# Transformer block on one core: row groups of the VectorE heads, measured matmul prices in the planner, and K/Q copies behind the LN roots

## The chip, the core and the metric

The kernel runs on one core of a Trainium2 chip. TensorE (PE) multiplies, ScalarE (ACT), VectorE (DVE) and GpSimd (POOL) work element by element, SyncE (SP) issues the DMAs. Each engine has its own instruction list, runs it in order and waits on semaphores for the others. The metric is the device time of one execution in microseconds, as a median of several runs.

## The reference

A block with layer norm ahead of attention, then layer norm ahead of a gated MLP, bfloat16 in and out, S = 2048, D = 640, 32 heads of 20, Df = 1728:

```
x  = A_x
h  = x + attention(layernorm(x)) @ wo      # softmax(q k^T / sqrt(20)) v, 32 heads
h2 = h + (gelu(n @ w_gate) * (n @ w_up)) @ w_down      # n = layernorm(h)
```

All 2048 queries see all 2048 keys, so there are 32 x 2048 x 2048 exponentials.

## The kernel before

**Tiles.** Heads go in 8 groups of 4, as a head of 20 (with its row for the bound, 21) fits a row group of 32 partitions. The queries are cut into 7 chunks (SIZES: 512, 512, 256, 256, 256, 128, 128). A chunk of 512 takes one head group per slot, a chunk of 256 two, a chunk of 128 four, so that there are 32 slots. The smallest piece of attention is a tile of 128 keys x 512 columns in one PSUM bank: `(slot, group, key block, j)`, where j is the head in its group and also the row group of PE that its score matmul uses (`qk_mms`, L934-935, `tile_position=(32 * j, 0)`). Tiles of unlike j can go through PE side by side, those of the same j can't.

**Units.** Tiles are laid out in one long list and cut into 703 units of two or three. The units use PSUM banks 0-2 and 3-4 in turns (0-2 and 3-5 in the second chunk). A unit is one group of score matmuls ("S", L935), one exponential on ACT over 1024 or 1536 columns (through the helper `I`, L354; the result goes into a ring of 18 probability tiles in pts and pts2), and later the products with V ("PV", L354, four column groups of PE, accumulated in bank 6).

**VectorE heads.** To spare ACT, some quads of four tiles (D_QUADS, 68 quads, 272 tiles) are taken out of the list. Their exponential is worked out on VectorE: `d_exp` copies the scores out of PSUM (L870) and runs six more passes over two or four tiles at a time. `dq` holds these tiles with the place from which each is due; D_PART says over which part of a head group they are spread in the first slots. The loop that makes the units takes the head of `dq` whenever it is due and ties it to the unit (`dtile`). In the second chunk it then has the third bank of the unit and sits in the same group of score matmuls. In the other chunks it has a spare bank and a matmul group of its own ("SD"), with the priority just behind the unit's scores. Its PV runs some units later, but before the last PV of its head group and slot.

**The order of work.** All engines' lists come out of `Sched.schedule` (from L91). It plays the program with a price for every operation (the third argument of `op`), a price for a change of array mode on PE (0.098 us) and of table on ACT (1.28), priorities, and the PSUM banks' owners. Whatever is ready with the best priority goes next. Ahead of the moment at which the next scores are due it keeps other work off PE (`due`, QK_LEAD). Where PE was too idle in its own reckoning it adds pad and warming matmuls. What comes out is a fixed order of instructions with waits. The prices themselves cost nothing on the chip, but they decide the order.

**Around attention.** First come the loads of x and the weights, LN1 (statistics on VectorE, for four row tiles of 128 on ACT; four square roots on ACT, each for four row tiles; the apply step on VectorE), PE transposes (L592) with copies to SBUF on ACT (L598) or VectorE (L601), and the projections of K, Q and V (matmuls in `chain`, L649; copies of K and Q on ACT at L682 or VectorE at L685, of V at L788 and L791). For the first head group the bound of the scores is found from the largest K (`top`, L677, then kd and sel0), multiplied by |Q| (L770) and added into Q (L774). Then the first scores can run. The other head groups are projected behind attention of the first chunk. After each chunk `post` runs the output projection, LN2, gate and up (L1107) with GELU, and down (L1164), as background behind the scores of the next chunk. The last chunk's `post` and what is left of the one before make up the end of the kernel.

Of the kernel before, what the change touches and what calls it, by code (L numbers as in the profile page):

```python
# [299 lines left out]
D = 640  # L300
# [4 lines left out]
NT = S // 128  # L305
NA = D // 128
NG = H // 4
SIZES = (512, 512, 256, 256, 256, 128, 128)
CHUNKS = tuple((sum(SIZES[:i]), n) for i, n in enumerate(SIZES))
# [14 lines left out]
D_FIRST, D_PART = 2, 0.75  # L324
# [5 lines left out]
P_QK, P_PV, P_PRO, P_EPI, P_LN, P_BG = 0, 1, 1.5, 2, 2.5, 3  # L330


def bass_sequential_preLN__mha_block__glu_gated_geglu__prompt_kernel(
# [12 lines left out]
    with ExitStack() as es:  # L346
# [184 lines left out]
        e_ops = []  # L531
        C_POOL, T_POOL, T_DVE = 0.9, (), (13, 15)

        def ln_stats(src, t, rkeys, prio, after=()):
            s = t % 4
            a = op("dve", I("bn_stats", stats[:, s, 0, :], src[:, 0:320]), 0.385, prio, reads=rkeys,
                   writes=[("st", s, 0)], after=after)
            b = op("dve", I("bn_stats", stats[:, s, 1, :], src[:, 320:640]), 0.385, prio, reads=rkeys,
                   writes=[("st", s, 1)], after=after)
            op("dve", I("bn_aggr", mv[:, t, :], stats[:, s, :, :]), 0.11, prio, reads=[("st", s, 0), ("st", s, 1)],  # L540
               writes=[("mv", t)])
            return [a, b]

        def ln_rsqrt(t0, n, prio, table=False, sqrt=False):
# [15 lines left out]
            if sqrt:  # L560
                op("act", I("activation", sd16[:, t0:t0 + n], sd16[:, t0:t0 + n], ACT.Sqrt), 0.2, 1, reads=[ks], writes=[ks])
# [26 lines left out]
        def transposes(src, rkeys, dst, wkey, banks, prio, evac, after=()):  # L588
# [8 lines left out]
            if evac == "act":  # L597
                op("act", lambda eng: eng.activation(dst, v(), ACT.Copy), c_act(D), prio, reads=[key],  # L598
                   writes=[wkey], rel=[bk], after=after)
            else:  # L600
                op("dve", lambda eng: eng.tensor_copy(dst, v()), c_dve(D, 0.54), prio, reads=[key], writes=[wkey],  # L601
# [45 lines left out]
        def chain(bk, key, n, steps, reads, prio, acq=True, after=()):  # L647
            for k, (l, r) in enumerate(steps):
                yield op("pe", lambda eng, l=l, r=r, k=k: eng.matmul(  # L649
                    bank(bk, n), l, r, start=(k == 0), stop=(k == len(steps) - 1)),  # L650
                    c_mm(n), prio, mode="full", util=n / 2400.0, reads=reads, writes=[key], acq=[bk] if (k == 0 and acq) else [],
# [17 lines left out]
        def proj_qk(col, t, c, dst, dkey, banks, prio, evac, after=(), peak=None):  # L669
# [6 lines left out]
            def top(src, r):  # L676
                return op("dve", lambda eng: eng.tensor_reduce(kd4[:, c:c + 1], src(), AX.X, ALU.max, apply_absolute_value=True),  # L677
                          c_dve(512), prio, reads=[r], writes=[("kd4", c)])
            if peak and c == 3:
# [11 lines left out]
        def proj_k(t, banks, prio, evac="dve"):  # L691
            for c in range(4):
                src = k_un[t % 2][:, 512 * c:512 * c + 512]
                proj_qk(D, t, c, src, ("ku", t % 2, c), banks, prio, evac, after=e_ops if t == 1 else (), peak=t == 0)
# [121 lines left out]
        PAT = [((0, 1, 2), (3, 4, 5)) if c in (1,) else ((0, 1, 2), (3, 4)) for c in range(len(CHUNKS))]  # L816
        units, ubank, dtile, begins = [], [], [], []
        i, di = 0, 0
        while i < len(tiles):
# [3 lines left out]
            if di < len(dq) and dq[di][0] <= i:  # L823
                xd = dq[di][1]
                di += 1
            n = len(bs) - (1 if six and xd else 0)
# [5 lines left out]
        assert di == len(dq)  # L832
# [17 lines left out]

        def d_exp(b, tile, prio, u):
# [5 lines left out]
            if h == 0:  # L857
                busy = set(x[1][1] for x in d_done)
                pool = [(kind, i) for i in range(5 if kind != "w" or slots[units[u][0][0]][0] > 3 else 3)]
# [8 lines left out]
            aft = tuple(e_ops) + (tuple(last_qk[0]) if c else ()) + (tuple(last_qk[1]) + tuple(d_late) if kind == "w" else ()) + \  # L868
                (tuple(last_qk[2]) + tuple(last_qk[3]) if kind == "w" and i[1] > 2 else ())
# [41 lines left out]
        def unit(u):  # L911
# [44 lines left out]
            elif xd:  # L956
                bd = Bank(*BG[slots[tl[0][0]][0]])
                qd = op("pe", [qk_mms(lambda: bank(bd), xd, kk) for kk in range(512 // CHUNKS[slots[xd[0]][0]][1])], 0.08,
# [50 lines left out]
        def base(c):  # L1009
            n = CHUNKS[c][1]  # L1010
            if n == 128:
                return 2 + (c == len(CHUNKS) - 1)
            return 2 * (c % 2) if n < 512 else 0
# [40 lines left out]
        def post(c, banks, tail):  # L1054
            p = P_EPI if tail else P_LN
# [5 lines left out]
            for tt in range(tb, tb + nt):  # L1061
# [8 lines left out]
                for hf in range(2):  # L1070
# [6 lines left out]
                       c_dve(320), p, reads=[key, ("h", tt, hf)], writes=[("h", tt, hf)], rel=[bk], after=first)  # L1077
# [179 lines left out]
```

## Time and profile before

| | |
|---|---|
| median of 3 runs | 921.31 us (921.13 to 921.42) |
| profiled execution | 921.06 us, its span 919.1 us (core 0, granted clock 1.000) |
| busy, share of the span | PE 92%, VectorE 86%, ACT 95%, GpSimd 5% |
| first exponential, last exponential begin | 35.42 us, 882.5 us |
| instructions | PE 10159 matmuls, VectorE 1456, ACT 787 |

The profile is of one execution, on the core that was traced. Busy time is the time in which an engine had at least one instruction at work; the rows of single groups give a mean duration, and as instructions overlap, their sum can be larger. The chain of work that ended last is followed back from the last instruction. In the timeline each line has the start (us), the length, the engine, the source line and the operation, with the number of instructions merged into it, and in brackets the idle time ahead of it and what ended that. PE's records contain matmuls that overlap; the distance from start to start tells what one costs.

### The profile page before, as it was taken

The page shows a single profiled execution, that of the slowest core. Times are in us where ns is not written, and L with a number is a line of the kernel's source. Part 1 is how long each engine was busy: PE and PEld are TensorE (multiplying, and loading weights), DVE is VectorE, ACT ScalarE, POOL GpSimd, SP SyncE. Part 2 cuts the span into 40 slices and gives each one's busy share as a digit, 9 for nine tenths or more (in the row PEclk, how much of TensorE's full clock was granted, in tenths as well). Part 3 has the DMA queues.
Part 4 walks back from the last instruction along what each step waited for, and adds up shares of the span by engine and source line. Part 5 has one row for each costly group of instructions (what it writes and reads, how often), then busy time and mean ns, then how long its engine had stood idle before and what let it go on. Part 6 is the DMA issues. An engine that isn't in the chain of part 4 may idle for free.

```text
span 919.1 us, 23058 instructions
## 1 busy us (share of the span) xinstructions
PE 846.4 (92%) x10159; PEld 355.6 (39%) x10159; DVE 794.5 (86%) x1456; ACT 877.0 (95%) x787; POOL 42.1 (5%) x121
## 2 busy tenths in 40 slices
PE   3999999999898987989998998999999999999998
PEld 1432323222232222223343333344444445666577
DVE  7779999999799996988888999899999988878763
ACT  6899999999999999999999999999999999999961
POOL 5000000000001000000001000000202000100200
PEclk9999999999999999999999999999999999999999
DMA  7211021234701000000111000010110001000000
GB/s 257 82 33 44 19 55 50 80 77 89 274 1 30 1 1 2 1 1 16 44 30 31 2 2 1 1 17 30 23 37 2 16 9 38 17 17 24 9 17 16
DMA packets 39516, 34.36 MB, mean 37 GB/s; under 512 B 19436, under 2 KB 36936, under 8 KB 39416
## 3 DMA queue, kind: packets, MB, share of 16 engines
q1 hardware_dynamic: 39416, 32.89, 12.9%
q8 instruction: 80, 1.31, 0.6%
q14 instruction: 20, 0.16, 0.1%
HBM read 20.12 MB, written 8.09 MB: 31 GB/s over the span
## 4 chain that ended last, share of the span: by engine, by line
ACT 62%; PE 27%; DVE 11%; issue 1%; DVEq 0%
ACT pts L354 39%; ACT rege L354 22%; PE ps L935 8%; PE ps L1107 6%; PE ps L354 5%; DVE qt_all L354 4%; PE ps L1164 4%; PE ps L649 3%; DVE qt_all L870 2%; ACT L354 1%; DVE rege L870 1%; DVE stats L354 1%; PE ps L592 1%; PE ps L1030 1%; DVE rege L354 1%
## 5 line engine op out<-in xcount | busy, mean ns | idle before, releaser
L354 ACT ACTIVATE pts<-ps 128x1536 bf16<-128x1536 f32 (+1 forms) x471 | 559.3, 1318 | 3.5 <-PE ps L935 1.5
L935 PE MATMUL ps<-qt_all,kt_all 32*128 32x256 bf16 (+2 forms) x3584 | 320.8, 288 | 37.7 <-ACT pts L354 22.3
L354 ACT ACTIVATE rege<-ps 128x1536 bf16<-128x1536 f32 (+1 forms) x232 | 285.2, 1317 | 2.6 <-PE ps L354 2.0
L935 PEld LDWEIGHTS ps<-qt_all,kt_all 32*128 32x128 bf16 x3584 | 104.3, 92 | 259.0 <-ACT pts L354 135.1
L354 DVE TENSOR_TENSOR qt_all<-qt_all 128x2048 f16<-128x2048 f16 (+3 forms) x186 | 174.9, 940 | 2.2
L1107 PE MATMUL ps<-rege,regw 128*128 128x256 bf16 (+2 forms) x980 | 160.9, 290 | 9.9 <-ACT rege L354 3.4
L354 PE MATMUL ps<-pts,v_all 128*21 128x256 bf16 (+2 forms) x2080 | 122.6, 290 | 0.0
L870 DVE TENSOR_SCALAR qt_all<-ps 128x512 int16<-128x512 f32 x128 | 87.6, 685 | 27.5 <-PE ps L935 27.0
L870 DVE TENSOR_SCALAR rege<-ps 128x512 int16<-128x512 f32 x128 | 87.5, 684 | 15.6 <-PE ps L935 13.9
L1107 PEld LDWEIGHTS ps<-rege,regw 128*128 128x128 bf16 x980 | 71.9, 97 | 70.6 <-issue 28.7
L354 PE MATMUL ps<-rege,v_all 128*21 128x256 bf16 (+2 forms) x1204 | 94.9, 295 | 0.3
L649 PE MATMUL ps<-regw 128*128 128x512 bf16 (+1 forms) x360 | 87.9, 353 | 1.1 <-DVE rege L870 0.6
L354 DVE TENSOR_SCALAR qt_all<-qt_all 128x1024 f16<-128x1024 int16 (+2 forms) x153 | 84.9, 559 | 1.8
L1164 PE MATMUL ps<-regw,rege 128*128 128x320 bf16 x448 | 79.0, 301 | 1.7 <-DVE rege L1153 0.6
L354 DVE TENSOR_TENSOR rege<-rege 128x1024 f16<-128x1024 f16 (+4 forms) x102 | 66.0, 657 | 1.0
L354 PE MATMUL ps<-kt_all,zer 128*32 128x512 bf16 x736 | 60.6, 384 | 0.0
L354 PEld LDWEIGHTS ps<-pts,v_all 128*21 128x21 bf16 x2080 | 44.9, 91 | 33.3 <-issue 29.3
L354 DVE TENSOR_SCALAR rege<-rege 128x1024 int16<-128x1024 int16 (+2 forms) x117 | 50.2, 447 | 1.1
L1164 PEld LDWEIGHTS ps<-regw,rege 128*128 128x128 bf16 x448 | 37.3, 97 | 33.9 <-issue 16.2
L1153 DVE TENSOR_TENSOR rege<-rege,ps 128x512 bf16<-128x512 bf16 (+1 forms) x53 | 35.7, 676 | 14.3 <-PE ps L1107 14.1
L649 PEld LDWEIGHTS ps<-regw 128*128 128x128 bf16 x360 | 29.2, 98 | 46.8 <-issue 24.8
L354 PEld LDWEIGHTS ps<-rege,v_all 128*21 128x21 bf16 x1204 | 32.4, 91 | 24.7 <-issue 16.8
(106 smaller groups left out, 564.9 us busy)
## 6 DMA issues: line engine op xcount, KB each, us to landing
rege<-in_A_x_dram SPq DMA_DIRECT2D x6, 640.0 KB, 5.2
q_rows<-regw SPq DMA_DIRECT2D x20, 128.0 KB, 1.7
out_dram<-rege SPq DMA_DIRECT2D x16, 160.0 KB, 1.8
regw<-in_B_w_gate_dram SPq DMA_DIRECT2D x1, 2160.0 KB, 12.8
regw<-in_B_w_up_dram SPq DMA_DIRECT2D x1, 2160.0 KB, 17.8
regw<-in_B_w_down_dram SPq DMA_DIRECT2D x1, 2080.0 KB, 22.9
kt_all<-k_rows SPq DMA_DIRECT2D x12, 160.0 KB
qt_all<-q_rows SPq DMA_DIRECT2D x12, 160.0 KB
```

The source lines that it names most:

```text
L354: return lambda eng: getattr(eng, method)(*args, **kwargs)
L592: op("pe", lambda eng, a=a: eng.transpose(bank16(bk, D)[:, 128 * a:128 * a + 128], src[:, a * 128:(a + 1) * 128], ident[:]), 0.055, prio, ...
L649: yield op("pe", lambda eng, l=l, r=r, k=k: eng.matmul(bank(bk, n), l, r, start=(k == 0), stop=(k == len(steps) - 1)), c_mm(n), prio, mode ...
L870: d_ops.append(op("dve", lambda eng: eng.tensor_scalar(v[:, 512 * h:512 * h + 512], bank(b), EXP_MUL, -32000.0, ALU.mult, ALU.max), c_dve( ...
L935: return lambda eng: eng.matmul(out()[:, kk * nq:(kk + 1) * nq], kt_all[32 * j:32 * j + 32, g, kt * 128:(kt + 1) * 128], qt_all[32 * j:32 ...
L1030: op("pe", lambda eng, tt=tt: eng.transpose(bank(b2)[:, tt * 128:(tt + 1) * 128], osb[:, s, tt * 128:(tt + 1) * 128], identf[:]), c_mm(128 ...
L1107: op("pe", lambda eng, a=a, f=f, fi=fi: eng.matmul(bank(bk)[:, fi * nq:(fi + 1) * nq], w[:, a, F0[f]:F0[f] + 128], hnT[:, a, 128 * tb:128 ...
L1153: hdone.append(op("dve", lambda eng, bu=bu, fv=fv, w=w: eng.tensor_tensor(fv, fv, bank(bu, w), ALU.mult), c_dve(w), p, reads=[ku] + hkeys( ...
L1164: op("pe", lambda eng, f=f, o=o, hf=hf, bk=bk: eng.matmul(bank(bk, 320), ha_f[:, o:o + 128], wd[:, f, hf * 320:(hf + 1) * 320], start=(f = ...
```

## The change

It has four parts.

1. The loop that makes the units looks at the next tiles of the same VectorE quad (up to four) and takes the first whose row group j none of the unit's tiles has; where none fits, the unit goes without and the tile stays in the queue. D_PART goes from 0.75 to 0.65.
2. Prices of the planner: 0.21 us for a VectorE score group on a taken row group and 0.01 on a free one, instead of 0.08 for both; LN statistics 0.41 and 0.12 instead of 0.385 and 0.11; copies of transposes on ACT 0.065 more, on VectorE 0.58 ns an element instead of 0.54; 0.1 us more for each matmul of the first projections (COLD); C_POOL is used by nothing, as T_POOL is empty.
3. K and Q copies of the first projections also wait for the first three of the four LN1 roots (`sqrts[:SQ]`).
4. Constants are put in place of expressions (BASE, SIX, q_done, P_LND, P_LNP, HOLD); they have the values that the expressions gave.

```diff
-D_FIRST, D_PART = 2, 0.75
+D_FIRST, D_PART = 2, 0.65
...
-        C_POOL, T_POOL, T_DVE = 0.9, (), (13, 15)
+        C_POOL, T_POOL, T_DVE = 1.9, (), (13, 15)
+        SQ, HOLD, COLD = 3, 0, 0.1
...
-            a = op("dve", I("bn_stats", stats[:, s, 0, :], src[:, 0:320]), 0.385, prio, reads=rkeys,
+            a = op("dve", I("bn_stats", stats[:, s, 0, :], src[:, 0:320]), 0.41, prio, reads=rkeys,
...
-                op("act", I("activation", sd16[:, t0:t0 + n], sd16[:, t0:t0 + n], ACT.Sqrt), 0.2, 1, reads=[ks], writes=[ks])
+                sqrts.append(op("act", I("activation", sd16[:, t0:t0 + n], sd16[:, t0:t0 + n], ACT.Sqrt), 0.2, 1, reads=[ks], writes=[ks]))
...
-                op("act", lambda eng: eng.activation(dst, v(), ACT.Copy), c_act(D), prio, reads=[key],
+                op("act", lambda eng: eng.activation(dst, v(), ACT.Copy), c_act(D) + 0.065, prio, reads=[key],
...
-                op("dve", lambda eng: eng.tensor_copy(dst, v()), c_dve(D, 0.54), prio, reads=[key], writes=[wkey],
+                op("dve", lambda eng: eng.tensor_copy(dst, v()), c_dve(D, 0.58), prio, reads=[key], writes=[wkey],
...
+            cold = COLD if prio == P_PRO and not any(("xnT", tt) in reads for tt in range(4, NT)) else 0.0
...
-                    c_mm(n), prio, mode="full", util=n / 2400.0, reads=reads, writes=[key], acq=[bk] if (k == 0 and acq) else [],
+                    c_mm(n) + cold, prio, mode="full", util=n / 2400.0, reads=reads, writes=[key], acq=[bk] if (k == 0 and acq) else [],
...
+            if prio == P_PRO:
+                after = tuple(sqrts[:SQ])
             if peak and c == 3:
                 after = (top(lambda: bank(bk), key),)
...
-            if di < len(dq) and dq[di][0] <= i:
-                xd = dq[di][1]
-                di += 1
-            n = len(bs) - (1 if six and xd else 0)
+            n = len(bs)
+            if dq and dq[0][0] <= i:
+                n -= 1 if six else 0
+                js = [x[3] for x in tiles[i:i + n]]
+                q = dq[0][1][:3]
+                fit = [k for k in range(min(4, len(dq))) if dq[k][1][:3] == q and dq[k][1][3] not in js]
+                if fit:
+                    xd = dq.pop(fit[0])[1]
+                elif six:
+                    n += 1
...
-                qd = op("pe", [qk_mms(lambda: bank(bd), xd, kk) for kk in range(512 // CHUNKS[slots[xd[0]][0]][1])], 0.08,
+                qd = op("pe", [qk_mms(lambda: bank(bd), xd, kk) for kk in range(512 // CHUNKS[slots[xd[0]][0]][1])],
+                        0.21 if xd[3] in [x[3] for x in tl] else 0.01,
                         P_QK + 0.5, mode="row", util=0.0533, reads=qk_reads(xd), writes=[("SD", xd)], acq=[bd], after=[qk])
```

The order in which instructions stand on each engine comes out of the planner, so nearly every line of each list moves. In the new order the counts are 765 ACT and 1456 VectorE instructions and 178 on SP, as before; PE has 10178 matmuls instead of 10159 (12 more pad matmuls and 7 more warming ones). The widths of the exponentials are the same in number (370 of 1536 columns, 333 of 1024). ACT loads its tables 16 times instead of 14.

## The prediction

> **What bounds the kernel now.** I read the page first (busy times, chain), then busy times by stage, then the timeline of each stage, and last the start times of single instructions.
>
> ```profile
> PE 846.4 (92%) x10159; PEld 355.6 (39%) x10159; DVE 794.5 (86%) x1456; ACT 877.0 (95%) x787; POOL 42.1 (5%) x121
> ACT 62%; PE 27%; DVE 11%; issue 1%; DVEq 0%
> ```
>
> ScalarE (ACT) is the busiest engine and holds most of the chain; TensorE (PE) comes next. The average hides three stages, cut here at the first and last exponential (us, then busy time of each engine):
>
> ```profile
> 0.00:35.42 35.42, 20.69 (x148) 11.68 (x148) 28.27 (x84) 25.79 (x48) 12.77 (x36) 1.00 0.54 182
> 35.42:882.50 847.08, 792.63 (x9583) 316.40 (x9583) 750.77 (x1337) 841.81 (x727) 29.30 (x85) 1.00 0.12 32
> 882.50:919.10 36.60, 33.09 (x430) 27.48 (x428) 15.51 (x36) 9.36 (x14) 0.00 (x0) 1.00 0.06 20
> ```
>
> In the middle ACT is busy 841.8 of 847.1 us, so PE's 792.6 matter only where a score group comes too late. At the end PE is the bound (33.1 of 36.6); at the start the chain changes engines.
>
> The busy time of the middle hides its waits, because exponentials overlap in the records (a 128x1536 one lasts 1.515 us). From start to start, one that waits for nothing takes 1.330 us (128x1536) or 0.904 (128x1024). Summed over the 697 neighbouring pairs, the trace has 18.1 us above that. This is the whole stock that a better PE order can win there.
>
> **Collisions.** The timeline of PE in the second chunk shows the price:
>
> ```profile
> 249.69 0.60 PE L935 MATMUL ps<-qt_all,kt_all 32*128 32x512 bf16 x3
> ...
> 251.26 0.39 PE L935 MATMUL ps<-qt_all,kt_all 32*128 32x512 bf16 x3
> ...
> 252.13 0.60 PE L935 MATMUL ps<-qt_all,kt_all 32*128 32x512 bf16 x3
> ```
>
> Three score matmuls on three row groups take 0.39 us. Where the VectorE head uses a row group that the unit already has, they take 0.60: +0.21. In the other chunks the VectorE score stands behind the unit's group. From the score group's start to the next instruction it is 0.53 us with a taken row group and 0.33 with a free one. Without a VectorE score it is 0.32. The planner counted 0.08 for all of these outside the second chunk, and nothing for the extra 0.21 inside it.
>
> From the lists of units, 171 of 272 VectorE scores collide before and none after. What PE gains:
> - second chunk: 37 x 0.21 = 7.8 us;
> - other chunks, scores directly behind their group: before 90 colliding x 0.213 + 53 free x 0.008 = 19.6; after 108 x 0.008 = 0.9;
> - other chunks, scores that the order puts further back, so that PE changes its array mode twice (0.318 each): before 62 = 19.7, after 96 = 30.5.
> Together 47.1 - 31.4 = 15.7 us less, with 2.2 us more of fillers (12 pad matmuls in 3 groups of 0.217; 7 warming ones of 0.216). So PE has 13.5 us less in all.
>
> What of it ACT sees is worked out from the 18.1 us, sorted by the unit that ends the pair's first exponential:
> - 171 colliding: 7.3 us, 0.043 each (0.090 in the second chunk);
> - 99 with a free row group: 1.97 us, 0.020 each;
> - 424 without a VectorE score: 5.0 us, 0.012 each;
> - 3 long waits of 0.81, 1.53 and 1.51 us, together 3.85 us.
> After, with 272 free and some 425 without, this gives 5.4 + 5.1 = 10.5, and 3.85 if the long waits stay: 14.3. **Term 1: -3.8 us.** Bounds: -16 (all lateness and all long waits go) and +4 (three more long waits). I take the class means, as the colliding and the free groups stand side by side in one trace.
>
> The long waits are another thing, seen in the list of waits:
>
> ```profile
> ACT rege L354 <- PE ps L354: 2.0, 2, 1.4
> ACT pts L354 <- PE ps L354: 1.4, 1, 1.4
> ```
>
> Here the scores were there (0.8 to 2.3 us before), but the exponential's slot in the ring of 18 probability tiles was not yet read by PV, as a head group's last PV also needs its VectorE heads. D_PART 0.65 issues those of the first eight head groups earlier, which should help; the new choice bunches heads, which should hurt. I count both at nothing and keep 3.85 each way for the range.
>
> **The start.** The timeline of ACT:
>
> ```profile
> 20.91 0.60 ACT L682 ACTIVATE regw<-ps 128x512 bf16<-128x512 f32 x1 [2.41 <-PE ps L649]
> 21.41 0.38 ACT L354 ACTIVATE sd<-sd 128x4 bf16<-128x4 bf16 x3
> 22.18 0.60 ACT L682 ACTIVATE regw<-ps 128x512 bf16<-128x512 f32 x1 [0.39 <-PE ps L649]
> ```
>
> ACT sat 2.41 us until the first K copy, and three roots (inputs ready at 20.45) ran behind it at 21.41. After, the K and Q copies wait for three of the four roots: two roots run before the first copy. Queued behind that copy are the fourth root, the next copy and the ten transposed tiles' copies; the first K copy itself isn't late, its PE chain ends at 20.9 and the roots take 0.2 us from 20.5. So VectorE's twelve remaining LN applies start some 1.3 us earlier than 22.83 and its top reduction (0.69), which stood ahead of them, goes behind eight of them. PE must follow: its transposes began at 23.47, right behind 24 projection matmuls. In the new order 17 stand there, and before the first score group there are 37 of 128x512 instead of 42, so 5 x 0.216 = 1.08 us go behind it. PE was busy from 18.56 to the first scores at 34.98 but for 0.24 us; with six 128x320 ahead instead of four that gap fills. VectorE's chain from the top reduction to the bound also loses one 0.69 us copy from its middle. **Term 2: -1.2 us** (bounds 0 and -1.8: nothing if a copy or transpose wait fills the hole; all of the gap, the 1.08 and part of the 0.69 otherwise). The five matmuls moved fall into the first chunk, where PE has 13.5 us less in the whole to do.
>
> [...] In this trace the 128x512 projections stand 0.42 us apart until 21.14 us and 0.216 after. [...]
>
> **The end.** Timeline of PE:
>
> ```profile
> 890.09 2.88 PE L1164 MATMUL ps<-regw,rege 128*128 128x320 bf16 x20
> 892.80 1.56 PE L1107 MATMUL ps<-rege,regw 128*128 128x128 bf16 x25
> 894.20 0.44 PE L592 MATMUL ps<-ident,xn_t 128*128 128x128 bf16 x5
> 894.48 8.82 PE L1107 MATMUL ps<-rege,regw 128*128 128x128 bf16 x152
> 903.13 3.97 PE L1164 MATMUL ps<-regw,rege 128*128 128x320 bf16 x28
> 906.94 4.80 PE L1107 MATMUL ps<-rege,regw 128*128 128x128 bf16 x83
> 912.32 3.98 PE L1164 MATMUL ps<-regw,rege 128*128 128x320 bf16 x28 [0.59 <-DVE rege L1132]
> ```
>
> PE works off a backlog of the two chunks before while the last chunk's LN, GELU and copies run beside it, so the end follows PE's count. Behind the last score group stand 267 gate and up matmuls of 128x128 (0.056 each) and 107 of 128x320 (0.136) before; after, 220 of 128x128, 36 of 128x256 (0.109) and 112 of 128x320. That is -2.6 + 3.9 + 0.7 = **term 3: +2.0 us** (bounds +1 and +3.5; below only if today's 1.2 us of gaps close). ACT gets two more table loads there (1.28 each), hidden: ACT is busy 9.4 of 36.6 us.
> The last exponential is 1.33 us long instead of 0.90, with as many of each in all, so its start and PE's last scores come 0.4 earlier: **term 4: -0.4.**
>
> The GELU blocks, their five pairs of table loads in the middle, all other durations and counts are the same: 765 ACT, 1456 VectorE, 178 SP instructions in both. The new planner prices for statistics and copies only reorder.
>
> **Sum.** 919.1 - 3.8 - 1.2 + 2.0 - 0.4 = 915.7 us of span; with the 1.96 us around the span (921.06 - 919.10) 917.7. The median of the runs is 0.25 above the profiled time, which I split: **917.8 us**.
>
> **Rivals.**
> 1. *Hidden anyway* (20%). PE isn't the bound of the middle, and 34 more VectorE scores stand apart from their group, each with 0.32 us of mode changes; if each delays the next scores by 0.1 us, that is 3.4 and term 1 is gone. Then -1.2 + 2.0 - 0.4 = +0.4: 921.5, up to 922.7 without term 2. For it: PE was idle for over 50 us of the middle already. Against: 0.043 against 0.020 us.
> 2. *VectorE late, ring waits* (16%, slower). A VectorE tile costs 0.685 for its copy and half of six passes (0.42 + 0.42 + 3 x 0.685 + 0.42), 2.3 us in all; a unit comes every 1.2 us. Stretches of four units with three or more such tiles number 30 before and 116 after. In them VectorE falls up to 2.2 us behind, the group's last PV waits, and the ring fills: 1.28 us for each such wait. With three more in place of term 1: +0.4 + 3.85, 925.5. It decides from two more on, if term 1 is missing. Against: 40 quiet stretches without any become 115, in which VectorE catches up.
> 3. *The forecast* (64%), between 914 and 919.4, including a start that does not move (918.9).
>
> **Numbers.** About 0.2% (1.8 us) is what a measurement of this kernel can tell from no change: faster 0.64, same 0.20, slower 0.16. The range takes in half of the long waits' 3.85 below and rival 1 and the mild part of rival 2 above: 913.5 to 923.0.
>
> **What would show it.** In the new profile no score line of the second chunk at 0.60; the first exponential near 34.2; the excess over 1.330 and 0.904 near 14 us, the two ring rows at most 4; PE's stretch behind the last scores near 36 us. A first exponential at 35.4, ring rows over 6 us, or transposes still waiting for VectorE near 23 would prove me wrong.

## The result and the profile after

The changed kernel takes **923.33 us** (median of 18 runs, 920.76 to 926.58) against 921.27 us for the kernel before, run beside it (18 runs, 920.35 to 921.89). The ratio is 1.0025 [1.0019, 1.0032]: it is slower. The forecast of 917.8 us named the wrong sign, and the time lies just above its range. The profiled execution took 923.23 us with a span of 921.2 us, 2.1 us more than before.

First the two lines of the page of the changed kernel (busy time of each engine; shares of the chain that ended last):

```profile
PE 836.2 (91%) x10178; PEld 355.1 (39%) x10178; DVE 794.8 (86%) x1456; ACT 880.7 (96%) x789; POOL 41.0 (4%) x121
ACT 56%; PE 28%; DVE 15%; issue 1%; POOL 1%; DVEq 0%; POOLq 0%
```

PE has 10.2 us less to do, as the change intends, and the kernel is not faster for it. The stages of the changed kernel, cut again at the first and last exponential, say where that went (stretch, its length, then busy time and instructions of PE, PEld, DVE, ACT, POOL, granted clock, DMA share, GB/s):

```profile
0.00:33.79 33.79, 19.35 (x143) 11.51 (x143) 27.88 (x83) 26.19 (x49) 12.82 (x36) 1.00 0.56 191
33.79:882.95 849.16, 782.12 (x9615) 314.88 (x9615) 750.61 (x1337) 842.03 (x727) 28.16 (x85) 1.00 0.12 32
882.95:921.20 38.25, 34.70 (x423) 28.66 (x420) 16.33 (x37) 12.48 (x16) 0.00 (x0) 1.00 0.06 19
```

The start is 1.6 us shorter, the end 1.7 us longer, and the middle 2.1 us longer (849.16 against 847.08), although PE is busy 10.5 us less in it (782.12 against 792.63). ACT's own busy time there did not move (842.03 against 841.81). So ACT waits or is held up more, while PE rests more.

The start times of the exponentials split the 2.1 us of span:

| | before | after | difference |
|---|---|---|---|
| first exponential begins | 35.42 | 33.79 | -1.64 |
| excess over 1.330 and 0.904 us, 697 pairs | 18.14 | 20.42 | +2.28 |
| five pairs with a GELU block between them | 42.50 | 43.12 | +0.62 |
| wide exponentials among the 697 pairs | 367 | 365 | 2 x 0.426 = -0.85 |
| last exponential's begin to the end | 36.61 | 38.28 | +1.67 |

What the change was made for is there. Score groups of the second chunk in the timeline of PE (start, length, engine, line, operation, instructions):

```profile
250.09 0.39 PE L951 MATMUL ps<-qt_all,kt_all 32*128 32x512 bf16 x3 [0.22 <-ACT pts L357]
...
251.12 0.39 PE L951 MATMUL ps<-qt_all,kt_all 32*128 32x512 bf16 x3
...
252.10 0.39 PE L951 MATMUL ps<-qt_all,kt_all 32*128 32x512 bf16 x3
```

Before, 37 groups of this chunk took 0.60 us; now none does. The excess in this chunk falls from 4.64 to 2.28 us. All other chunks together lose 4.6 us: 13.5 becomes 18.1.

The next fence is the timeline of PE in the fourth chunk, at a place where ACT comes 0.31 us late:

```profile
604.06 0.61 PE L951 MATMUL ps<-qt_all,kt_all 32*128 32x256 bf16 x6
604.60 0.99 PE L1179 MATMUL ps<-regw,rege 128*128 128x320 bf16 x6
605.52 0.39 PE L951 MATMUL ps<-qt_all,kt_all 32*128 32x256 bf16 x6
...
606.09 0.39 PE L951 MATMUL ps<-qt_all,kt_all 32*128 32x256 bf16 x2
606.41 0.31 PE L1179 MATMUL ps<-regw,rege 128*128 128x320 bf16 x1
606.65 0.39 PE L951 MATMUL ps<-qt_all,kt_all 32*128 32x256 bf16 x4
```

Six matmuls on three row groups take 0.39 us (605.52). The group at 604.06 has as many and takes 0.61: two tiles of one unit and, directly behind, the VectorE tile of an *earlier* unit on a row group that is taken. The choice freed each VectorE tile of its own unit's row groups; where the order put it behind another's, it collides again. At 606.09 a VectorE tile stands alone between background matmuls: it changes the array mode twice, and 0.32 us pass until the next matmul begins (606.41). The planner counted 0.01 us for the first of these, and for the second 0.01 and 0.098 for each of the two changes of mode.

The last thing that is new is the granted clock. Stretches of the changed kernel around the GELU blocks of two chunks (columns as above):

```profile
717.40:720.80 3.40, 1.77 (x16) 0.94 (x16) 3.15 (x9) 3.39 (x4) 0.00 (x0) 0.99 0.02 5
720.80:724.20 3.40, 3.25 (x37) 1.56 (x41) 1.38 (x3) 3.24 (x4) 0.00 (x0) 0.51 1.02 96
...
795.90:799.30 3.40, 1.23 (x18) 0.81 (x19) 3.40 (x9) 3.39 (x3) 2.96 (x6) 0.99 0.00 0
799.30:802.70 3.40, 3.40 (x18) 2.40 (x17) 2.38 (x3) 3.37 (x4) 1.48 (x3) 0.51 0.02 5
```

For 3.41 us from 720.74 and from 799.24 PE ran at half clock (granted clock 0.50). Before, there was no such stretch between the first and the last exponential. Ahead of each PE had waited for a GELU block:

```profile
796.32 0.66 PE L1044 MATMUL ps<-identf,osb 128*128 128x128 f32 x4
799.10 5.01 PE L1122 MATMUL ps<-rege,regw 128*128 128x256 bf16 x29 [2.12 <-ACT rege L357]
```

29 gate and up matmuls of 128x256 take 5.01 us instead of 29 x 0.109 = 3.2.

### The profile page after: what moved, and what is told of

It reads as the page before. It is cut to its first block, busy times and chain, and to the rows that moved or that the text cites. A ratio compares the mean times of both kernels' runs of the same rounds, so it can differ in the third digit from the quotient of the medians.

```text
span 921.2 us, 23123 instructions
## 1 busy us (share of the span) xinstructions
PE 836.2 (91%) x10178; PEld 355.1 (39%) x10178; DVE 794.8 (86%) x1456; ACT 880.7 (96%) x789; POOL 41.0 (4%) x121
## 4 chain that ended last, share of the span: by engine, by line
ACT 56%; PE 28%; DVE 15%; issue 1%; POOL 1%; DVEq 0%; POOLq 0%
ACT pts L357 35%; ACT rege L357 20%; PE ps L951 8%; PE ps L357 5%; PE ps L1122 5%; PE ps L654 5%; DVE qt_all L357 4%; PE ps L1179 4%; DVE rege L357 3%; DVE qt_all L886 2%; DVE rege L886 1%; ACT L357 1%; DVE stats L357 1%; PE ps L1044 1%; DVE regw L692 1%
## 5 line engine op out<-in xcount | busy, mean ns | idle before, releaser
L357 ACT ACTIVATE pts<-ps 128x1024 bf16<-128x1024 f32 (+1 forms) x472 | 559.9, 1326 | 5.8 <-PE ps L951 2.6
L951 PE MATMUL ps<-qt_all,kt_all 32*128 32x256 bf16 (+2 forms) x3584 | 307.5, 289 | 45.3 <-ACT pts L357 26.7
L357 ACT ACTIVATE rege<-ps 128x1024 bf16<-128x1024 f32 (+1 forms) x231 | 287.0, 1337 | 1.8 <-PE ps L951 1.3
L951 PEld LDWEIGHTS ps<-qt_all,kt_all 32*128 32x128 bf16 x3584 | 99.7, 92 | 271.1 <-ACT pts L357 140.0
L357 DVE TENSOR_TENSOR qt_all<-qt_all 128x2048 f16<-128x2048 f16 (+3 forms) x186 | 175.1, 941 | 2.4
L357 PE MATMUL ps<-pts,v_all 128*21 128x256 bf16 (+2 forms) x2070 | 123.2, 291 | 0.0
L357 PE MATMUL ps<-rege,v_all 128*21 128x256 bf16 (+2 forms) x1214 | 93.9, 294 | 0.7 <-DVE rege L357 0.3
L357 DVE TENSOR_SCALAR qt_all<-qt_all 128x1024 f16<-128x1024 int16 (+2 forms) x153 | 85.1, 562 | 1.9
L357 DVE TENSOR_TENSOR rege<-rege 128x1024 f16<-128x1024 f16 (+4 forms) x102 | 66.4, 657 | 1.0
L357 PE MATMUL ps<-kt_all,zer 128*32 128x512 bf16 x748 | 60.9, 384 | 0.0
L357 PEld LDWEIGHTS ps<-pts,v_all 128*21 128x21 bf16 x2070 | 45.3, 91 | 32.2 <-issue 27.9
L357 DVE TENSOR_SCALAR rege<-rege 128x1024 int16<-128x1024 int16 (+2 forms) x117 | 49.6, 444 | 0.7
L357 PEld LDWEIGHTS ps<-rege,v_all 128*21 128x21 bf16 x1214 | 32.5, 91 | 22.7 <-issue 15.0
```

Source lines behind the costliest of these rows:

```text
L357: return lambda eng: getattr(eng, method)(*args, **kwargs)
L951: return lambda eng: eng.matmul(out()[:, kk * nq:(kk + 1) * nq], kt_all[32 * j:32 * j + 32, g, kt * 128:(kt + 1) * 128], qt_all[32 * j:32 ...
```

## The experiments

**Theory A**: a VectorE score that doesn't stand directly behind its own unit's scores costs ACT time, and the price of 0.01 us makes the planner place more of them so, and at worse moments. **Theory B**: with PE less busy, its clock halves behind some gaps, and that costs what the choice won. **Rivals**: VectorE comes late and the ring of probability tiles fills (the prediction's second rival); the start's gain is given back in the first chunk; or any other order of this planner varies as much.

All runs in one table. "Plain" is the excess of pairs that are not a long wait (over 0.45 us) and not in a half-clock stretch. The first column is the median of several runs, the others come from one profiled execution each (us). Line numbers in the fences are those of each kernel's own text: the helper I is L354 before, L357 after and L364 in experiments 3, 5, 11 and 12.

Three things limit what a row says. The profiled execution isn't always near the median: it was the slowest one in experiments 8 (932.52 us) and 10 (933.47), and the fastest one in 3 (922.26) and 7 (923.16), so the column of half-clock stretches shows one execution. In chunks 3 to 7 not all orders are different ones: PE's list in experiment 1 is that of before, with 9 nearly the same; that of 3 is that of 5, with 12 nearly the same; and 6 has that of the changed kernel with 12 more matmuls. The same list gave 6.7 and 6.6, 5.5 and 4.9, 8.5 and 8.7 us, so differences of 0.6 us are no more than two executions of one order show. In experiment 4 only four GELU blocks lie in the middle.

| kernel | median, ratio to before | first exp. | plain, chunk 1 | plain, chunk 2 | plain, chunks 3-7 | long waits | half clock | GELU pairs | last exp. to end |
|---|---|---|---|---|---|---|---|---|---|
| before | 921.1 to 921.5 | 35.5 | 2.9 | 4.2 | 6.7 | 4.3 | 0 | 42.5 | 36.6 |
| after | 923.33, 1.0025 | 33.8 | 3.7 | 2.3 | 8.5 | 4.2 | 1.7 | 43.1 | 38.2 |
| 1 start alone | 922.77, 1.0015 | 33.0 | 2.9 | 4.0 | 6.6 | 7.8 | 1.7 | 42.5 | 36.6 |
| 2 choice and its prices alone | 927.15, 1.0060 | 34.4 | 4.1 | 1.8 | 8.3 | 3.4 | 5.3 | 43.2 | 38.2 |
| 3 apart priced, all chunks | 922.86, 1.0023 | 33.1 | 1.6 | 2.3 | 5.5 | 10.9 | 0 | 44.4 | 36.5 |
| 4 more fillers | 945.89, 1.0263 | 33.8 | 5.9 | 2.2 | 14.0 | 13.6 | 1.5 | 35.7 | 51.0 |
| 5 apart priced, chunks 2-7 | 916.65, 0.9952 | 33.1 | 3.7 | 2.3 | 4.9 | 3.1 | 1.7 | 44.4 | 36.5 |
| 6 warming before GELU | 921.37, 1.0015 | 33.1 | 3.7 | 2.3 | 8.7 | 3.1 | 1.5 | 43.1 | 38.2 |
| 7 choice, price 0.08 | 924.74, 1.0040 | 35.6 | 2.4 | 2.0 | 6.6 | 7.0 | 0 | 44.8 | 37.3 |
| 8 after, 0.011 for 0.010 | 928.09, 1.0081 | 33.1 | 3.7 | 2.3 | 9.5 | 4.5 | 8.0 | 42.2 | 40.9 |
| 9 before, 0.081 for 0.080 | 922.86, 1.0021 | 35.1 | 3.0 | 3.6 | 6.6 | 7.4 | 0 | 42.5 | 36.6 |
| 10 after without the start | 931.58, 1.0107 | 35.6 | 3.3 | 2.2 | 11.8 | 9.0 | 3.9 | 42.6 | 37.0 |
| 11 as 5 with 0.21 | 918.07, 0.9960 | 33.1 | 3.7 | 2.3 | 4.9 | 3.5 | 3.1 | 44.2 | 35.4 |
| 12 as 5 without the start | 923.36, 1.0021 | 35.5 | 3.3 | 2.1 | 5.1 | 3.6 | 4.2 | 44.4 | 36.5 |

**1. The start alone** (before, with the third part of the change and COLD).

```diff
+            if prio == P_PRO:
+                after = tuple(sqrts[:SQ])
...
-                    c_mm(n), prio, mode="full", util=n / 2400.0, reads=reads, writes=[key], acq=[bk] if (k == 0 and acq) else [],
+                    c_mm(n) + cold, prio, mode="full", util=n / 2400.0, reads=reads, writes=[key], acq=[bk] if (k == 0 and acq) else [],
```

> The kernel before with only the start's part (K and Q copies behind three roots, 0.1 us more for the first projections' matmuls). Its order behind the first chunk is that of before: same 267 + 107 matmuls behind the last scores. If the start is the only part that pays: first exponential near 33.8 us as in the changed kernel (before 35.47), the excess of the exponentials near 18 us, no half-clock window in the middle, time about 1.6 us less than before, 919.7. Rival: the moved projections delay the first chunk and the 1.6 are given back: 921.3.

922.77 us, ratio 1.0015 [1.0005, 1.0024], more than either case had. The first exponential begins 2.5 us earlier (some of it isn't the order's, as term 2 below shows), and 3.0 us are lost behind the sixth exponential. Timeline of PE and then of ACT in this kernel:

```profile
41.96 0.61 PE L354 MATMUL ps<-pts,v_all 128*21 128x512 bf16 x8 [0.27 <-DVE v_all L795]
```

```profile
42.63 2.37 ACT L354 ACTIVATE pts<-ps 128x1536 bf16<-128x1536 f32 x2 [2.82 <-PE ps L354]
```

The first PV waits for VectorE's copy of V. Until it has run, the exponentials' slots aren't free, and ACT sits 2.82 us. By itself the start is given back at the next thing that is late. In the changed kernel the first PV runs at 38.17 us, and the same wait isn't there.

**2. The choice with its two prices alone** (before, with the new loop and its two prices).

```diff
-            if di < len(dq) and dq[di][0] <= i:
+            if dq and dq[0][0] <= i:
...
+                fit = [k for k in range(min(4, len(dq))) if dq[k][1][:3] == q and dq[k][1][3] not in js]
...
+                        0.21 if xd[3] in [x[3] for x in tl] else 0.01,
```

> The kernel before with only the choice of free row groups and the two prices 0.21 and 0.01. Theory A (the price 0.01 is also charged to VectorE scores that don't follow their own unit's scores, which cost 0.32 or, behind another unit's scores on the same row group, 0.54): second chunk better by about 2 us, all other chunks together worse by 3 to 5 us, the tail 2 us longer: 923 to 925. Theory B (half-clock windows of PE alone make the loss): mean granted clock under 0.998 and the excess, the pairs in such windows left out, well under 18 us. If the choice pays as forecast: 919 or less.

927.15 us, 1.0060 [1.0042, 1.0079], more than theory A had. The second chunk gains (1.8 us plain), chunks 3 to 7 lose (8.3), and four half-clock stretches cost 5.3 us. The larger loss is in this part of the change, not in the start.

**3. A price for VectorE scores that stand apart.** The planner gives a VectorE score 0.22 us unless PE's last operation was its own unit's score group. Only the order differs, and with it the planner's fillers (10244 matmuls instead of 10178).

```diff
+                if o.tag and o.tag[0] == "SD":
+                    o.dur = 0.01 if last_qk == o.qk else 0.22
+                if o.tag and o.tag[0] == "S":
+                    last_qk = o.i
+                elif e == "pe":
+                    last_qk = None
```

> The changed kernel with one more rule in the planner: a VectorE score group is priced 0.01 only where it goes directly behind its own unit's scores, else 0.22. The order is planned anew, and 111 instead of 96 stand apart. Theory A: excess of the pairs with a VectorE score apart falls from 0.082 us each to 0.03 or less, the whole excess from 20.4 to about 14 to 16 us, time about 918 to 920. Theory B (half-clock windows): no change beyond the number of such windows, 1.2 us each; 922 to 924.

922.86 us, 1.0023 [1.0013, 1.0032]: no gain on the whole. Chunks 3 to 7 fall to 5.5 us plain and there is no half-clock stretch, but one wait takes 7.5 us. Timeline of SP's queue and of ACT:

```profile
133.89 0.35 SPq L364 DMA_DIRECT2D q_rows<-regw  x1
...
138.03 0.57 SPq L364 DMA_DIRECT2D qt_all<-bounds  x1
```

```profile
143.75 3.28 ACT L364 ACTIVATE pts<-ps 128x1024 bf16<-128x1024 f32 x3 [7.10 <-PE ps L958]
```

The first chunk's background also holds the projections of the later head groups. The fifth group's query rows go out at 133.89 us instead of 124.32 in the changed kernel. That dearer VectorE scores leave less room for this background is likely, but not shown. The scores that need them start at 143.3.

**4. More fillers** (the changed kernel with fuller windows in the planner's own reckoning).

```diff
-WARM_WIN, WARM_MIN = 3.4, 0.5
+WARM_WIN, WARM_MIN = 3.4, 0.65
...
-PAD_WIN, PAD_MIN = 3.4, 0.42
+PAD_WIN, PAD_MIN = 3.4, 0.55
```

> The changed kernel with higher thresholds for the planner's fillers (0.65 for 0.5 and 0.55 for 0.42 of a 3.4 us window): 1775 filler matmuls for 800. Theory B: mean granted clock back to 0.999, no half-clock window in the middle; if these windows are what the change lost, the time falls by 2 to 3 us to about 920.5. Theory A: the clock is back but the fillers push background work behind the last scores (384 gate and up matmuls instead of 256), so the tail is some 10 us longer, and the excess of the middle stays near 18 us: 928 to 934.

945.89 us, 1.0263 [1.0246, 1.0280]. There is still one half-clock stretch. The fillers push background out of the middle: 384 gate and up matmuls stand behind the last scores, and the end takes 51.0 us. It says little of theory B, as it moves everything.

**5. The price of experiment 3 from the second chunk on.**

```diff
-                if o.tag and o.tag[0] == "SD":
+                if o.tag and o.tag[0] == "SD" and o.late:
...
+                sc.ops[qd].qk, sc.ops[qd].late = qk, slots[tl[0][0]][0] > 0
```

> The changed kernel, with the price 0.22 for VectorE scores that don't follow their own unit's scores directly, but only from the second chunk on, so that the first chunk keeps the order of the changed kernel and not the late group of e3. Theory A: first chunk as in the changed kernel (first exponential 33.8, excess 6.3 us), chunks 3 to 7 with an excess of about 6 to 7 us (e3 6.3, changed kernel 11.8 with its half-clock windows, before 8.2), last exponential to end 36.5 us (38.2): span 914 to 917, time 916 to 919, faster than both. Theory B (half-clock windows alone): no gain but by their number; 921 to 923.

**916.65 us** (915.98 to 917.54), 0.9952 [0.9937, 0.9966]: faster than both kernels. Its stages:

```profile
0.00:33.09 33.09, 18.52 (x141) 11.33 (x143) 27.69 (x83) 26.20 (x49) 12.80 (x36) 1.00 0.58 195
33.09:879.09 846.00, 774.80 (x9642) 317.74 (x9697) 751.11 (x1339) 841.20 (x728) 27.77 (x85) 1.00 0.12 32
879.09:915.60 36.51, 32.64 (x397) 26.55 (x394) 14.82 (x35) 8.11 (x13) 0.00 (x0) 1.00 0.06 19
```

The middle is 846.00 us, 3.2 less than the changed kernel's, with the same choice of tiles. Chunks 3 to 7 have 4.9 us plain against 8.5 and 6.7. Scores standing apart cost 0.046 us each (60) instead of 0.082 (56), those behind another unit's 0.025 (28) instead of 0.050 (29). So it isn't their number that fell, but they stand where they hurt less; what makes such a place is not shown. Of the 5.6 us by which this profile's span is shorter than the changed kernel's, 3.6 are the plain excess of chunks 3 to 7, 1.7 the end, 1.1 the long waits and 0.7 the first exponential; the GELU pairs take 1.2 back.

**6. Warming ahead of two GELU gaps.** The changed kernel's order to the instruction, with 12 more warming matmuls at two places near 715 and 796 us.

```diff
+            if o.tag == "warm" and o.fns == [sc.warm] and seen in (572, 637):
+                o.fns = [sc.warm] * 7
```

> The changed kernel in the very same order; only two warming matmuls, ahead of the GELU gaps at 713.6 and 795.3 us, are done seven times each (12 more matmuls of 0.216 us, while ACT runs GELU). Theory B: the half-clock window at 799 goes and the one at 721 comes less often; mean clock 0.998 or more in most executions, 1 to 2.4 us faster than the changed kernel: 921 to 922.3. Its rest of excess (about 18 us) stays. Theory A alone (half clock costs nothing, as ACT is the bound): 923.3 as the changed kernel.

921.37 us, 1.0015 [1.0000, 1.0030], 2.0 us under the changed kernel's median. The stretches at the same gaps:

```profile
715.60:719.00 3.40, 2.33 (x18) 1.46 (x17) 3.40 (x7) 3.38 (x3) 0.00 (x0) 1.00 0.00 0
719.00:722.40 3.40, 2.34 (x26) 1.27 (x25) 2.85 (x7) 3.39 (x4) 0.00 (x0) 1.00 0.79 43
797.50:800.90 3.40, 2.35 (x20) 1.87 (x20) 3.40 (x8) 3.38 (x3) 2.71 (x4) 1.00 0.02 5
800.90:804.30 3.40, 2.30 (x36) 1.47 (x35) 3.36 (x8) 3.39 (x4) 0.00 (x0) 1.00 0.08 17
```

The clock stays at 1.00 where it was 0.51. This profile has one half-clock stretch elsewhere (483.4), which the profile of the changed kernel hadn't. At these two places theory B holds for the clock. That it holds for the time, the runs support: 7 of these 10 executions took at most 921.83 us, with a mean clock of 0.998 or 1.000, against 2 of 18 of the changed kernel; the others have a lower mean clock (0.996, 0.994, 0.987) and took 923.4, 924.0 and 927.7 us. The size is less sure: the medians differ by 2.0 us, the means by 1.0, and the intervals of the two ratios overlap.

The changed kernel's 18 runs point the same way: at a mean clock of 0.998 they took 920.8 to 922.0 us (3 runs), at 0.996 922.5 to 923.4 (7), at 0.994 923.5 to 924.1 (5), at 0.991 926.2 to 926.6 (3). One stretch of 3.41 us at half clock takes 0.0019 off the mean, so an estimate from these runs is 1.2 us for each. The only execution of this order without a stretch is one of experiment 6: 921.03 us, as the kernel before (921.12 beside it).

**7. The choice at the old price** (before, with the new loop of experiment 2 and the price as it was).

```diff
+                fit = [k for k in range(min(4, len(dq))) if dq[k][1][:3] == q and dq[k][1][3] not in js]
```

> The kernel before with the choice of free row groups but the old price 0.08 for every VectorE score. Theory A: the price is nearer to what a score set apart costs (0.32 with its mode changes), so the pairs with one apart lose less than the 0.082 us each of the changed kernel, about 0.05 to 0.06; chunks 3 to 7 about 8 to 10 us of excess against 13.7 in e2; but 70 ns too much for each of 100 that follow directly, spent as idle. Behind the last scores stand 70 + 261 gate and up matmuls: the tail is 5 us longer than in the changed kernel. 924 to 928.

924.74 us, 1.0040 [1.0026, 1.0054]. Chunks 3 to 7 fall back to 6.6 us plain, so in this term the price of 0.01 did the harm, not the choice. The profiled execution has no half-clock stretch and is the fastest (923.16 us); the other four, at a mean clock of 0.996, took 924.7 to 924.9. The first chunk has 7.0 us of long waits, the GELU pairs take 2.3 us more than before and the end 0.7. And 6.6 is no less than the 6.7 of the kernel before: outside the second chunk, freeing the row groups without an order that uses it gains nothing.

**8. A price moved by a thousandth** (the changed kernel).

```diff
-                        0.21 if xd[3] in [x[3] for x in tl] else 0.01,
+                        0.21 if xd[3] in [x[3] for x in tl] else 0.011,
```

> The changed kernel with 0.011 instead of 0.010 for a VectorE score on a free row group; nothing else. The planner gives another order from the sixth head group or so on. If the price itself mattered by its size, the time would be that of the changed kernel within 0.3 us. If the order is a lottery in details (which GELU gap, which background matmul stands before which score group), it moves by 1 to 4 us either way; with fewer gate and up matmuls behind the last scores (244 for 256) the tail is about 3 us shorter, 36.5 or less: 919 to 923.

928.09 us, 1.0081 [1.0053, 1.0110]: 4.8 us more than the changed kernel, and outside the expected range. In the profiled execution, the slowest of four, half-clock stretches cost 8.0 us in the middle. But the one run with a mean clock of 0.998 still took 925.93 us, where the changed kernel took 920.8 to 922.0, so half clock isn't all of it.

**9. The same with the kernel before.**

```diff
-                qd = op("pe", [qk_mms(lambda: bank(bd), xd, kk) for kk in range(512 // CHUNKS[slots[xd[0]][0]][1])], 0.08,
+                qd = op("pe", [qk_mms(lambda: bank(bd), xd, kk) for kk in range(512 // CHUNKS[slots[xd[0]][0]][1])], 0.081,
```

> The kernel before with the planner's price of a separate VectorE score group at 0.081 us for 0.080: same choice, same start, same work behind the last scores, only a slightly other order (3 more of its scores stand apart from their unit's). It asks how much a meaningless step of a price moves the kernel before, as 0.011 for 0.010 moved the changed one by 4.8 us. If the price of 0.010 is what made the changed kernel's order fragile: within 1.5 us of before, 920 to 923. If any order of this planner varies by some us: 918 to 926, with the difference in first-chunk ring waits or in half-clock windows.

922.86 us, 1.0021 [1.0011, 1.0030], with 3.1 us more of long waits in the first two chunks and nothing else of note. A step of a price that means nothing moves the kernel before by 1.7 us, nearly as much as the change did (2.1).

**10. The changed kernel without its start part.**

```diff
-        SQ, HOLD, COLD = 3, 0, 0.1
+        SQ, HOLD, COLD = 0, 0, 0.0
```

> The changed kernel without its start part: K and Q copies wait for no LN1 root and COLD is 0; choice and prices stay. 47 projection matmuls of 128x512 stand before the first scores again, 204 VectorE scores outside the second chunk of which 107 are apart, and behind the last scores there are 40 more of 128x128, 36 fewer of 128x256 and 21 fewer of 128x320, so the tail should be 40 x 0.056 - 36 x 0.109 - 21 x 0.136 = 4.5 us shorter, near 33.7. Theory that the start is worth its 1.6 us: first exponential near 35.4; excess of the exponentials 20 to 22; time 923.3 + 1.6 - 4.5 + 0 to 1.5 = 920.4 to 922. Rival, that the start part is given back in the first chunk: first-chunk excess falls below 5 and the time is 919 or less.

931.58 us, 1.0107 [1.0089, 1.0124]. Both cases are missed: the first exponential is at 35.6 as expected, but long waits rise by 4.8 us, half-clock stretches by 2.2, chunks 3 to 7 by 3.3. The end is 37.0, not 33.7: it isn't PE's count alone.

**11. Experiment 5 with 0.21 for 0.22.**

```diff
-                    o.dur = 0.01 if last_qk == o.qk else 0.22
+                    o.dur = 0.01 if last_qk == o.qk else 0.21
```

> The version that priced VectorE scores not directly behind their own unit's scores at 0.22 us from the second chunk on (median 916.65), with 0.21 for 0.22. If that price is the cause of the gain: excess of chunks 3 to 7 stays at 6 to 8.5 us, tail near 36, half-clock windows at most one, time 915.5 to 919. If the 916.65 was one lucky order among many: chunks 3 to 7 at 10 us or more, or new ring waits, and the time 920 or more.

918.07 us, 0.9960 [0.9945, 0.9975]. Chunks 3 to 7 plain are 4.9 us again; with three half-clock stretches instead of one (at most one was expected). PE's list in chunks 3 to 7 is clearly another one than in experiment 5, so the gain isn't one lucky order.

**12. Experiment 5 without the start part** (the edit of experiment 10 on experiment 5).

```diff
-        SQ, HOLD, COLD = 3, 0, 0.1
+        SQ, HOLD, COLD = 0, 0, 0.0
```

> The same version with 0.22, without the start part (no wait for the roots, COLD 0): the choice of row groups with a price for standing apart. The work behind the last scores is the same to a matmul. If the start part is worth what its first exponential shows (2.3 us in that version): first exponential near 35.4, the rest the same, time 918.5 to 919.5. If the start is given back in the first chunk, as it was alone: first-chunk excess 2 us lower and time 916 to 917.5. In both cases below the kernel before (921.2), which the row groups with a right price then give by themselves.

923.36 us, 1.0021 [1.0012, 1.0031]. Its median isn't below before, as both cases had it. Chunks 3 to 7 plain stay low (5.1 us), the first exponential is 2.3 us later, and half-clock stretches take 4.2 us instead of 1.7. Nine of its ten executions have a mean clock of 0.994; the only one at 1.000 took 920.43 us, 0.75 below before. So the row groups with the higher price don't make up for what else the order does; without the start the gain of experiment 5 isn't seen.

**What the twelve say together.** Chunks 3 to 7, plain: the six kernels with 0.01 wherever the tile stands (after, 2, 4, 6, 8, 10) have 8.3 to 14.0 us. The four with 0.08 (before, 1, 7, 9) have 6.6 to 6.7, and the four that price standing apart (3, 5, 11, 12) have 4.9 to 5.5. The three classes don't overlap. Three pairs differ in the price alone: 0.08 to 0.01 with the same choice (7 to 2) goes from 6.6 to 8.3 us; 0.01 to 0.22 where a score stands apart goes from 8.5 to 4.9 (after to 5) and from 11.8 to 5.1 (10 to 12). For this term theory A is shown as to 0.01; the lead of the third class over 0.08 (1.2 to 1.8 us) rests on two really different orders on each side. The price that wins is not the measured one: with the two changes of mode the planner counts 0.22 + 2 x 0.098 = 0.42 us for a score that stands alone, where PE loses 0.318 by the timeline of the kernel before.

Theory B is shown for the clock where it was tried, at two places, and is worth some 1 to 2 us there. The time as a whole needs more than these: long waits (3.1 to 13.6 us) and half-clock stretches (0 to 8.0) vary from order to order and can hide both. Which small difference of the order makes them is open.

## Why the prediction was wrong

**Term 1 is the step that failed**: "After, with 272 free and some 425 without, this gives 5.4 + 5.1 = 10.5." It took the mean of the 99 free scores of the kernel before, 0.020 us, for all 272 after, and gave the new order, which the price of 0.01 makes, no cost of its own. By the place of the VectorE score that PE has between the score groups of the pair's two units, the two kernels have:

| place of the VectorE score | before: pairs, mean, sum (us) | after: pairs, mean, sum (us) |
|---|---|---|
| third bank of its unit, second chunk | 67, 0.059, 3.96 | 68, 0.026, 1.76 |
| directly behind its own unit's scores | 141, 0.020, 2.87 | 108, 0.029, 3.14 |
| directly behind another unit's, taken row group | 10, 0.014, 0.14 | 29, 0.050, 1.45 |
| apart from any scores | 45, 0.059, 2.68 | 56, 0.082, 4.61 |
| none | 426, 0.011, 4.65 | 430, 0.015, 6.41 |
| long waits that ended on a PV (ring) | 3, 1.28, 3.85 | 4, 0.76, 3.05 |

After, together 20.4 us, half-clock stretches included (1.7), against the 14.3 forecast. (A pair with scores of two kinds counts as apart; the few pairs left have no excess.) The 261 pairs with a VectorE score cost 11.0 us, 0.042 each: as much as a colliding one before (0.043), where 0.020 was forecast.

Two things are in this. The mean of 0.020 mixed places: of the 99 free scores before, 51 stood directly behind their own unit's scores (0.011), 30 in the third bank (0.020) and 13 apart (0.057). But with before's figures for each place the counts of after would give 11.0 us and, with 3.85 of ring waits, 14.8, so the mix alone is 0.5 us. The greater part is that the same places cost more in the new order: 0.082 for 0.059 apart, 0.050 for 0.014 behind another unit, 0.029 for 0.011 behind its own. Experiment 5 has the same choice of tiles and as many scores apart, and they cost 0.046; so what a place costs depends on the order around it, and the price of 0.01 made the worse order.

The prediction had the sign of this in its own PE sum ("before 62 = 19.7, after 96 = 30.5") and dropped it in the step from PE to ACT. That sum has an error of its own: of the 96, 38 stand directly behind another unit's scores on a taken row group, which changes no array mode, but collides (0.61 us instead of 0.39 at 604.06 above). This could have been read from the order; "171 of 272 VectorE scores collide before and none after" is not so on PE.

- **Second chunk**: right. The 37 groups of 0.60 us are gone (37 x 0.21 = 7.8 us of PE), and ACT's excess is 2.4 us less.
- **PE's sum** (13.5 us less): near. The middle shows 10.5 less busy time. But spare time on PE was no gain; at two places a gap came ahead of a half-clock stretch.
- **Rival 1**, "if each delays the next scores by 0.1 us, that is 3.4 and term 1 is gone", had the right mechanism in part: 0.082 us is close to its 0.1. It missed the collisions with other units and that the other places got dearer too, and stopped at 921.5 to 922.7, as the half-clock stretches weren't in it.
- **Rival 2**, VectorE late and the ring full: not the cause. The long waits that ended on a PV fell from 3.85 to 3.05 us. The list of waits of the changed kernel for ACT's ring slots (total, times, longest) has no long one:

```profile
ACT pts L357 <- PE ps L357: 2.4, 4, 0.9
```

- **Term 2, the start**: -1.6 against -1.2, near. Timeline of ACT:

```profile
19.97 0.34 ACT L357 ACTIVATE sd<-sd 128x4 bf16<-128x4 bf16 x2 [0.96 <-DVE sd L357]
21.04 0.60 ACT L689 ACTIVATE regw<-ps 128x512 bf16<-128x512 f32 x1 [0.73 <-PE ps L654]
21.53 0.20 ACT L357 ACTIVATE sd<-sd 128x4 bf16<-128x4 bf16 x1
```

Two roots now run before the first K copy, which is not much later (21.04 for 20.91), as forecast. The first exponential also moves from execution to execution: experiment 6, in the changed kernel's order, has it at 33.00 instead of 33.79. There PE's full clock begins at 19.19 us, in the profile of the changed kernel at 21.00 (the 128x512 projections stand 0.427 us apart up to there, 0.216 behind it). The two profiles compared here are alike in this (21.12 before), so the 1.6 us stand; the 2.5 us of experiment 1 (full clock from 19.64) shrink to 2.1 against experiment 9, which has before's start (35.04, full clock from 19.97).

- **Term 3, the end**: +1.67 against +2.0, near, and PE is busy 1.61 us more there. The same way of counting missed by 3.3 us in experiment 10. **Term 4**, the last exponential's width: two wide exponentials leave the 697 pairs (-0.85 us), one of them into a GELU pair (+0.43): -0.4, as forecast. What is left of the GELU pairs' difference is +0.2.
- **The clock**: the prediction looked at it in the first microseconds only (0.42 us from one projection to the next until 21.14 us, 0.216 after). The profile of the kernel before has no half clock in the middle, and that a change which takes 13.5 us of work from PE might bring it there wasn't weighed. In the profile of the changed kernel the two stretches hold 1.7 us of the 6.1 by which term 1 was missed.
- **The range** missed by 0.3 us. It let the VectorE scores gain or nothing; the bound of +4 for term 1 was there but stood for long waits alone. (Its other bound, -16, is no sum of the rows named: all of them make 18.1.)

## What to carry to other kernels

A class mean holds for the order it was measured in. When a change moves instructions, cut the classes by what stands next to them on the engine, not by what they belong to, and still expect another order to change what each place costs. A price in a planner that is right for one place and used for all makes the wrong place look cheap. Where a planner's order varies by 2 to 5 us with a thousandth of a price, compare the term that the change aims at over several orders before believing in the total of one.

## What the runs showed of the hardware

In the middle of the changed kernel, where PE is busy 782.12 of 849.16 us, its granted clock is 0.50 for 3.41 us at a time. From 21.00 us, where the record of full clock begins, the two stretches begin 699.73 and 778.24 us later, at 720.74 and 799.24: 78.51 us apart, which is 23 times 3.4133, and 205 and 228 times 3.4133 behind the start. The profiles of three experiments show the same: in experiment 6 the stretch at 483.45 us begins 136.0 such steps behind the start of full clock (19.19), in experiment 1 the one at 299.60 us 82.0 steps behind it (19.64), and in experiment 2 four begin at 298.20, 509.90, 670.30 and 803.40 us, 62.0, 47.0 and 39.0 steps apart.

In the 3.41 us ahead of the two stretches of the changed kernel PE was busy 1.77 and 1.20 us. Busy time in the records doesn't settle when the clock falls: in experiment 12 PE was busy 2.03, 1.93 and 2.95 us in the 3.41 us up to the stretches at 459.70, 487.10 and 620.20, while in experiment 7 it was busy 1.68 us in such a step from 560.87, and the granted clock stayed at 1.00. What does settle it, the runs don't show.
